# Hash attention and a PReLU feed-forward block: the weights' loads move from SyncE's queue to GpSimd's

## The chip, the cores and the metric

The kernel runs on one core of a Trainium2 chip. The metric is the device time of one execution in microseconds; less is better. Times stated without a source are positions in one profiled execution, counted from the first instruction of its span.

## The reference, cut to what matters

Two blocks follow each other: attention in which a query sees only the keys whose six hash bits equal its own, and a feed-forward block with a leaky activation (one slope per hidden unit).

```python
q_bits = (np.einsum('bhsd,dk->bhsk', q, proj) > 0)      # k_bits likewise; 6 bits each
mask = q_bucket[:, :, :, None] == k_bucket[:, :, None, :]
scores = np.where(mask, scale * (q @ k.T), -1e9)        # batch 4, heads 8, seq 768, head_dim 64
attn = softmax(scores) @ v                              # reshaped to x: 3072 x 512
h = x @ w_in                                            # 512 x 2048
out = (np.maximum(h, 0) + alpha * np.minimum(h, 0)) @ w_out   # 2048 x 512
```

The two weight matrices and alpha come as 64-bit floats; q, k, v and proj are 32-bit.

## The kernel before, in words

**Attention, up to about 326 us.** The 32 heads are handled in 16 pairs. For each pair the kernel brings q and k into a layout with head_dim on the partitions (`qT`, `kT`): the first pair by transposes on TensorE (`turn`, L695), all later ones by VectorE (`turn_blocks`, L704), from loads in four blocks for each of q and k (`load_blocks`, L512). It computes the hash bits (`hash_bits`, L730, L736), whose results GpSimd copies by DMA to their places in `qb` and `kb` (L741, L743). Then come 12 score cells (`scores`, L768): each is two small matmuls on bits and two on values, into one of three PSUM buffers of the tag "sc", followed by an exponential on ScalarE (L771) into `pt`. TensorE then multiplies with v (`attend`, L801) and sums up denominators (`totals`, L815) from `accd`. VectorE adds the exponentials up (L779 to L790) for that, and divides (`divide`: L831 reads the sums, L843 and L849 form x, which is stored to `x_s` by L850). GpSimd moves four small pieces of reciprocals in between (L840, L841).

**Weights, beside attention.** The 32 pieces of the two weight matrices, 128 x 512 elements of 64 bits (512 KB), are loaded during attention, two for each pair, and turned into 32-bit floats. `load_weight(i)` (L578 to L582) issues the load into one of three buffers (tag "raw", `bufs=3`). `weight_abs(i)` (L596 and L600 on ScalarE, or L598 on VectorE) reads it first, then `weight_clamp` and `weight_parts` (L606, L612), and `weight_sum` (L637, L640) is its last reader, so that a buffer comes free when L637 ends. `weight_group` stores finished pieces (`w_out_r`, L651) or combines four of them on GpSimd (L659, begun by a small copy to `late_sum`, L676) and stores them (`w_in_s`, L664).

**Feed-forward, from about 326 us to the end.** Matmuls of seven products per step (`Product`, L902), with weights and x read back from DRAM by SyncE (L864, L880, L979). Early in this part GpSimd loads and stores eight pieces `wo` of 512 KB (L989, L996).

**What sets the order.** Instructions wrapped in `do(...)` keep program order on their engine. DMA issues are placed by the scheduler; each engine's queue is then worked off in order, so that one whose buffer is not free holds all those behind it. The chain of calls around the change in each round `pi` (`i = 2 * pi`) is: scores, `divide` of the pair before, `weight_sum(i)`, `load_weight(i + 3)`, `weight_sum(i + 1)`, `load_weight(i + 4)`, hash bits of the next pair, `attend`, `totals`, `weight_abs(i + 2)`, loads of the pairs ahead, `weight_abs(i + 3)`. On ScalarE both `weight_abs` stand before the exponentials of the next pair. Ahead of the loop, `load` of the second pair's q and k (L1148, L1149) comes before `load_weight(0)` (L1150), and `weight_abs(0)` before the rest of the first pair's scores. In SyncE's queue before the change all q, k, v blocks but four, the weights' loads and all stores of the attention part stand in one row.

Of the kernel before, what the change touches and what calls it, by code (L numbers as in the profile page):

```python
# [349 lines left out]
def kernel(  # L350
# [48 lines left out]
    keep = ctx.enter_context(tc.tile_pool(name="keep", bufs=1))  # L399
    flag = keep.tile([1, 1], mybir.dt.int32, name="flag")  # L400
    fast_path(*args, flag)
    again = tc.nc.values_load(flag[0:1, 0:1])
    with tc.If(again > 0):
# [4 lines left out]
def fast_path(  # L408
# [12 lines left out]
    nc = tc.nc  # L421
# [61 lines left out]
    def load(pi, name):  # L483
        b, hp = pairs[pi]
        src = {"q": q, "k": k, "v": v}[name]
        if name == "v":
            t = pool.tile([P, 2, NC * D], F32, name=f"vn{pi}", tag="vn")
            nc.sync.dma_start(t, src[b, 2 * hp : 2 * hp + 2].rearrange("h (p c) d -> p h (c d)", c=NC))
            nat[name, pi] = t
        elif pi and name in BY_BLOCKS:  # L490
            load_blocks(pi, name)
        else:
            load_part(pi, name, slice(0, NC), nc.sync)

    def load_part(pi, name, cs, queue):
        b, hp = pairs[pi]
        src = {"q": q, "k": k}[name]
        if cs.start == 0:
            nat[name, pi] = pool.tile([P, NC, 2, D], F32, name=f"{name}n{pi}", tag=f"{name}n", bufs=3)
        for s in range(2):  # L500
            queue.dma_start(nat[name, pi][:, cs, s], src[b, 2 * hp + s].rearrange("(p c) d -> p c d", c=NC)[:, cs])
# [3 lines left out]
    def load_blocks(pi, name):  # L505
        b, hp = pairs[pi]
        src = {"q": q, "k": k}[name]
        nat[name, pi] = t = pool.tile([P, NC * 4, 32], F32, name=f"{name}n{pi}", tag=f"{name}n", bufs=3)
        for s in range(2):
            for h in range(2):  # L510
                a = D * s + 32 * h
                nc.sync.dma_start(  # L512
                    t[a : a + 32].rearrange("i (c u) d -> i c u d", u=4),
                    src[b, 2 * hp + s, :, 32 * h : 32 * h + 32].rearrange("(u i c) d -> i c u d", u=4, c=NC),
                )
# [39 lines left out]
    raw, wx, wr = {}, {}, {}  # L555
# [3 lines left out]
    def piece(i):  # L559


        if i < HW:
            n, m = divmod(i, 4)
            c, kk = divmod(n, 2)
            o, j = kk + 2 * (m // 2), c + 2 * (m % 2)
            return moe_w_in[o * P : (o + 1) * P, j * 512 : (j + 1) * 512]
        n, m = divmod(i - HW, 2)
        o = n + NI * m
        return moe_w_out[o * P : (o + 1) * P]
# [5 lines left out]
        ahead = (i + 1) * HW // TURNS > HW - len(left[0])  # L575
        order.append(left[0 if left[0] and ahead or not left[1] else 1].pop(0))

    def load_weight(i):  # L578
        if i < NW:
            i = order[i]  # L580
            raw[i] = pool.tile([P, 512], moe_w_in.dtype, name=f"raw{i}", tag="raw", bufs=3)
            nc.sync.dma_start(raw[i], piece(i))  # L582

    def halves(i):
        words = raw[i].bitcast(U32).rearrange("p (f t) -> p f t", t=2)
# [97 lines left out]
    def two_banks(name):  # L683
        return psum.tile([P, 2, 512], F32, name=name, tag="sc", bufs=3)
# [3 lines left out]
    def turn(pi, name, halves=BOTH, engine=None):  # L688

        src = nat[name, pi].rearrange("p c h d -> p c (h d)")  # L690
        if halves.start == 0:
            tr[name, pi] = pool.tile([P, S], F32, name=f"{name}T{pi}", tag=f"{name}T")
        ps = two_banks(f"tp_{name}{pi}")
        for c in range(CH * halves.start, CH * halves.stop):
            do(PE.transpose(ps[:, c // CH, c % CH * P :][:, :P], src[:, c], ident))  # L695
        dst = tr[name, pi].rearrange("p (h w) -> p h w", h=2)[:, halves]
        if engine is DVE:
            do(DVE.tensor_copy(dst, ps[:, halves, :CW]))
        else:
            do(ACT.activation(dst, ps[:, halves, :CW], AF.Copy, scale=DOWN if name == "q" else 1.0))  # L700
# [12 lines left out]
    def hash_bits(pi, halves=BOTH, engine=None):  # L713

        if halves.start == 0:
            bits["q", pi] = qbs[pi % 2]
            kb = pool.tile([P, 3 * CW], BF16, name=f"kb{pi}", tag="kb", bufs=1)
            bits["k", pi] = kb[:, :S]  # L720
            bits["raw", pi] = kb.rearrange("p (a w) -> p a w", w=CW)
        ps = {"k": two_banks(f"hs{pi}")}
        ps["q"] = psum_av.tile([P, 2, 512], F32, name=f"hsq{pi}", tag="av") if engine is DVE else ps["k"]
        for half in range(halves.start, halves.stop):
            for name in "qk" if engine is DVE else "kq":
                for s in range(2):
                    r, c = D * s, D * (s ^ half) + 32 * "kq".index(name)

                    for t, c in [("k", c)] + ([("q", c ^ D)] if engine is DVE and name == "q" else []):
                        do(PE.matmul(  # L730
                            ps[t][c : c + 32, half if t == "k" or engine is not DVE else 0, :CW], wh[r : r + D],
                            tr[name, pi][r : r + D, half * CW : (half + 1) * CW], start=True, stop=True,
                        ))
        if engine is None:
            raw = bits["raw", pi]
            do(ACT.activation(raw[:, 0:3:2], ps["k"][:, :, :CW], AF.Sign, bias=hb))  # L736
            for half in range(2):
                for s in range(2):
                    c = D * (s ^ half)
                    cols = slice(half * CW, (half + 1) * CW)  # L740
                    nc.gpsimd.dma_start(bits["q", pi][D * s : D * s + 32, cols], raw[c + 32 : c + 64, 2 * half])  # L741
                    if half:
                        nc.gpsimd.dma_start(bits["k", pi][D * s : D * s + D, cols], raw[c : c + D, 2])  # L743
            return
        for half in range(halves.start, halves.stop):
            cols = slice(half * CW, (half + 1) * CW)
            for s in range(2):
                c = D * (s ^ half ^ (engine is DVE)) + 32
                do(ACT.activation(
                    bits["q", pi][D * s : D * s + 32, cols], ps["q"][c : c + 32, 0 if engine is DVE else half, :CW], AF.Sign, bias=hb[c : c + 32],  # L750
                ))

            for to, c, n in [(0, 0, P)] if half == 0 else [(0, D, D), (D, 0, D)]:
                dst, src = bits["k", pi][to : to + n, cols], ps["k"][c : c + n, half, :CW]
                do(DVE.tensor_scalar(
                    dst, src, hb_k[c : c + n, 0:1], hb_k[c : c + n, 1:2], op0=ALU.is_gt, op1=ALU.subtract,
                ))
# [384 lines left out]
    for half in (first, second):  # L1142
        turn(0, "q", half)
        turn(0, "k", half, DVE)
        if half is first:
            nil[0]()
            hash_bits(0, first, DVE)
    load(1, "q")  # L1148
    load(1, "k")  # L1149
    load_weight(0)  # L1150
    load(0, "v")
    for i in range(1, 3):
        load_weight(i)
# [14 lines left out]
    for pi in range(NPAIR):  # L1168
        i = 2 * pi
# [13 lines left out]
        weight_sum(i)  # L1183
        weight_group(i)
        load_weight(i + 3)
        if pi == 0:
            weight_abs(1, DVE)
# [136 lines left out]
```

## Time and profile before

| | |
|---|---|
| median of 3 runs | 882.17 us (881.49 to 883.12) |
| the profiled execution's own time | 882.06 us |
| its span, first to last instruction | 880.2 us |
| busy TensorE matmul / weight load | 863.0 us (98%) / 576.0 us (65%) |
| busy VectorE | 749.2 us (85%) |
| busy ScalarE | 368.0 us (42%) |
| busy GpSimd | 96.8 us (11%) |
| mean granted TensorE clock | 0.993 |
| DMA moved | 137.23 MB, 156 GB/s over the span |
| share of the DMA engines' time, q1 (SyncE) / q0 (GpSimd) / q10 (ScalarE) | 49.5% / 3.9% / 0.5% |
| weights' loads | 32 from SyncE, 512 KB each, landing 3.7 to 7.1 us after issue, median 4.8 |
| hash bits' copies from GpSimd | 90, of 24 or 48 KB, landing 1.6 to 5.8 us after issue |
| an ordinary pair of the attention part | 19.15 us |

How to read it: PE is TensorE, DVE VectorE, ACT ScalarE, POOL GpSimd, SP SyncE; a "q" behind the name (SPq) is the engine's instruction queue, where DMAs are issued. A name such as L768 is a line of the kernel, and "sc<-qT,kT" is output and inputs by the program's names. The idle time before an instruction is put down to the one whose end released it. The DMA share is the mean busy share of the core's 16 DMA engines, and can exceed 1 where packets overlap.

### The profile page before, as it was taken

How to read it: one execution, taken by the hardware profiler on the slowest of the kernel's cores; microseconds unless marked ns; L12 is line 12 of the kernel's file. 1: busy time of each engine (PE TensorE's matmuls, PEld its weight loads, DVE VectorE, ACT ScalarE, POOL GpSimd, SP SyncE). 2: the span in 40 equal slices, each digit the busy share in tenths (PEclk: the TensorE clock that was granted, in tenths of full speed). 3: DMA queues.
4: the chain of work that ended last, by engine and by line, in shares of the span. 5: the costliest groups of instructions: out<-in, count | busy, mean ns of one | idle time of the engine just before them, and what ended most of it. 6: DMA issues, size and time to landing. Idle time of an engine off the chain costs nothing.

```text
span 880.2 us, 15210 instructions
## 1 busy us (share of the span) xinstructions
PE 863.0 (98%) x5706; PEld 576.0 (65%) x5706; DVE 749.2 (85%) x1215; ACT 368.0 (42%) x654; POOL 96.8 (11%) x220
## 2 busy tenths in 40 slices
PE   8999999999998999999999999999999999999996
PEld 3444444444443445559996558996557997557996
DVE  5999999999997978899888769898668988668986
ACT  6886888887766752221112222112222112222111
POOL 1221423323322311120000000000000000000000
PEclk9999999999998999999999999999999999999998
DMA  8866797797796347586433425334434333520242
GB/s 197 183 152 136 181 241 157 169 253 192 177 252 169 118 150 263 203 303 223 133 132 90 172 86 197 115 113 125 141 123 155 136 123 96 177 86 1 96 151 69
DMA packets 170819, 137.23 MB, mean 156 GB/s; under 512 B 126016, under 2 KB 154384, under 8 KB 167152
## 3 DMA queue, kind: packets, MB, share of 16 engines
q1 hardware_dynamic: 163136, 123.64, 49.5%
q0 software_dynamic: 5184, 11.34, 3.9%
q10 hardware_dynamic: 2416, 1.18, 0.5%
q8 instruction: 47, 0.77, 0.4%
q14 instruction: 36, 0.29, 0.1%
HBM read 104.87 MB, written 28.31 MB: 151 GB/s over the span
## 4 chain that ended last, share of the span: by engine, by line
PE 92%; DVE 3%; DMA 2%; issue 1%; ACT 1%; SPq 1%; ACTq 0%; DVEq 0%
PE sc L768 15%; PE av L801 13%; PE f_0a L902 2%; PE z_4a L902 2%; PE z_7a L902 2%; PE z_3a L902 2%; PE z_6a L902 2%; PE z_5a L902 2%; PE z_1a L902 2%; PE z_2a L902 2%; PE f_4a L902 2%; PE f_7a L902 2%; PE f_6a L902 2%; PE f_5a L902 2%; PE f_3a L902 2%; PE f_2a L902 2%
## 5 line engine op out<-in xcount | busy, mean ns | idle before, releaser
L771 ACT ACTIVATE pt<-sc 128x768 f32<-128x768 f32 x192 | 154.0, 812 | 8.3 <-PE sc L768 6.8
L768 PE MATMUL sc<-qT,kT 64*128 64x384 f32 x768 | 157.3, 488 | 0.0
L801 PE MATMUL av<-pt,vn 128*32 128x385 f32 (+1 forms) x1536 | 127.4, 486 | 0.0
L801 PEld LDWEIGHTS av<-pt,vn 128*32 128x32 f32 x1536 | 48.7, 109 | 77.5 <-issue 69.3
L768 PEld LDWEIGHTS sc<-qT,kT 64*128 64x128 f32 x768 | 69.3, 190 | 38.4 <-issue 38.1
L768 PE MATMUL sc<-qb,kb 64*128 64x384 bf16 x384 | 63.8, 328 | 8.0 <-ACT pt L771 7.0
L955 DVE TENSOR_TENSOR g<-g,g 128x384 f32<-128x384 f32 x128 | 68.3, 554 | 2.2
L1019 DVE TENSOR_TENSOR gs<-g,gs 128x768 f32<-128x768 f32 x56 | 53.3, 951 | 1.0
L1011 DVE TENSOR_TENSOR ws<-wl 128x512 f32<-128x512 f32 x56 | 38.4, 686 | 18.2 <-DMA wl<-w_out_s 16.3
L1019 DVE TENSOR_TENSOR gs<-g 128x768 f32<-128x768 f32 x56 | 53.2, 951 | 0.0
L596 ACT ACTIVATE wr<-raw 128x512 int32<-128x512 uint32 x32 | 22.1, 692 | 59.1 <-issue 30.2
L741 POOL DMA_DIRECT2D qb<-kb x60 | 30.1, 505 | 146.3 <-ACT kb L736 146.3
L768 PEld LDWEIGHTS <-kb 64*128 64x128 bf16 x384 | 19.6, 95 | 38.7 <-issue 14.1
L779 DVE TENSOR_TENSOR accp<-pt,pt 128x1536 f32<-128x1536 f32 x16 | 28.2, 1760 | 17.9 <-ACT pt L771 17.9
L951 DVE SCALAR_TENSOR_TENSOR g<-h,alpha 128x384 f32<-128x384 f32 x32 | 19.7, 616 | 25.2 <-ACT h L944 25.1
L784 DVE TENSOR_TENSOR accd<-accd,pt 128x1536 f32<-128x1536 f32 x16 | 28.1, 1758 | 1.7
L790 DVE TENSOR_TENSOR accd<-accd,accp 128x1536 f32<-128x1536 f32 x16 | 28.1, 1758 | 0.6
L787 DVE TENSOR_TENSOR accp<-accp,pt 128x1536 f32<-128x1536 f32 x16 | 28.0, 1753 | 0.0
L783 DVE TENSOR_TENSOR accd<-pt,pt 128x1536 f32<-128x1536 f32 x16 | 28.0, 1750 | 0.0
L902 PE MATMUL f_0a<-x,wi 128*128 128x384 f32 x64 | 23.5, 489 | 0.0
L902 PE MATMUL f_1a<-x,wi 128*128 128x384 f32 x64 | 23.3, 486 | 0.0
L902 PE MATMUL f_2a<-x,wi 128*128 128x384 f32 x64 | 23.3, 486 | 0.0
(355 smaller groups left out, 1740.2 us busy)
## 6 DMA issues: line engine op xcount, KB each, us to landing
wi<-w_in_s SPq DMA_DIRECT2D x32, 896.0 KB, 4.7
wl<-w_out_s SPq DMA_DIRECT2D x16, 1024.0 KB, 4.8
wl<-w_out_r SPq DMA_DIRECT2D x12, 1024.0 KB, 5.0
raw<-in_moe_w_out_dram SPq DMA_DIRECT2D x16, 512.0 KB, 4.9
raw<-in_moe_w_in_dram SPq DMA_DIRECT2D x16, 512.0 KB, 4.5
w_in_s<-wsi SPq DMA_DIRECT2D x16, 448.0 KB, 5.7
qn<-in_q_dram SPq DMA_DIRECT2D x64, 96.0 KB, 5.4
vn<-in_v_dram SPq DMA_DIRECT2D x16, 384.0 KB, 5.6
```

Of the source, the lines that this page charges most:

```text
L741: nc.gpsimd.dma_start(bits["q", pi][D * s : D * s + 32, cols], raw[c + 32 : c + 64, 2 * half])
L768: do(PE.matmul(sc[:, s, :CW], what["k", pi][r, ks], what["q", pi][r, qs], start=first, stop=not first,))
L771: do(ACT.activation(pts[kc][:, g, :, :CW], sc[:, :, :CW], AF.Exp, scale=SCALE / DOWN))
L779: do(DVE.tensor_tensor(accp[pi], p(0), p(1), op=ALU.add))
L783: do(DVE.tensor_tensor(accd[pi], p(3), p(4), op=ALU.add))
L784: do(DVE.tensor_tensor(accd[pi], accd[pi], p(5), op=ALU.add))
L790: do(DVE.tensor_tensor(accd[pi], accd[pi], accp[pi], op=ALU.add))
L801: do(PE.matmul(av[pi][D * s + t : D * s + t + 32, g, :w], nat["v", pi][:, s, kc * D + t : kc * D + t + 32], pts[kc][:, g, s, :w], start=(k ...
L902: do(PE.matmul(self.ps[bank], self.left(left, k), self.right(right, k), start=start and k == 0, stop=k == self.nk - 1, skip_group_check=no ...
L955: do(DVE.tensor_tensor(new_g(b, to)[:, i], g_m[b, x][:, i], g_m[b, y][:, i], op=ALU.subtract))
L1011: do(DVE.tensor_tensor(t, w2[b, n, x], w2[b, n, y], op=op))
L1019: do(DVE.tensor_tensor(t, g2[b, n, x], g2[b, n, y], op=ALU.subtract))
```

## The change

`load_weight` gets a parameter for the issuing engine, with GpSimd as its default. The first weight's load is issued by SyncE and stands before the loads of the second pair's blocks of q and k; it stood behind them. All other weights' loads keep their place in the program and go to GpSimd's queue.

```diff
-    def load_weight(i):
+    def load_weight(i, queue=nc.gpsimd):
         if i < NW:
             i = order[i]
             raw[i] = pool.tile([P, 512], moe_w_in.dtype, name=f"raw{i}", tag="raw", bufs=3)
-            nc.sync.dma_start(raw[i], piece(i))
+            queue.dma_start(raw[i], piece(i))
...
+    load_weight(0, nc.sync)
     load(1, "q")
     load(1, "k")
-    load_weight(0)
     load(0, "v")
     for i in range(1, 3):
         load_weight(i)
```

In the changed program, GpSimd's queue has 31 more DMA issues and SyncE's 31 fewer; TensorE, VectorE and ScalarE have the same instructions in the same order. In GpSimd's queue the loads 1, 2 and 3 stand after its memsets and before the first hash-bit copies; later the load `i + 3` stands before the six hash-bit copies of a round, and the load `i + 4` after them.

## The prediction

> **What bounds the kernel now.** I read five views: the busy shares, TensorE's waits, the chain of waits, the stretches pair by pair, and the timeline of each engine around what they showed. TensorE is busy 863.0 of 880.2 us, so little can be gained outside its idle time, and its waits are few (columns: who waited, for whom, total us, times, longest):
>
> ```profile
> PE sc L768 <- ACT pt L771: 7.0, 2, 4.3
> PE sc L768 <- DVE st L831: 1.0, 2, 0.8
> ACT wr L596 <- DMA raw<-in_moe_w_out_dram: 11.8, 2, 9.1
> ```
>
> ScalarE takes its work in order: the conversion of a raw weight (L596) stands before the exponentials (L771) which free TensorE's score banks. Twice the weight is late, and exponentials and scores wait behind it. The timeline shows both (start, duration, in brackets the idle time before):
>
> ```profile
> 15.23 0.67 ACT L596 ACTIVATE wr<-raw 128x512 int32<-128x512 uint32 x1 [2.68 <-DMA raw<-in_moe_w_out_dram]
> 16.65 0.34 PE L768 MATMUL sc<-qb,kb 64*128 64x384 bf16 x2 [2.68 <-ACT pt L771]
> ...
> 267.15 0.66 ACT L596 ACTIVATE wr<-raw 128x512 int32<-128x512 uint32 x1 [9.10 <-DMA raw<-in_moe_w_out_dram]
> 269.11 0.51 PE L768 MATMUL sc<-qb,kb 64*128 64x384 bf16 x2 [4.28 <-ACT pt L771]
> ```
>
> Why the second weight is late is in SyncE's queue. Its buffer was free at 251.4, when VectorE ended L637 (started 250.71), but SyncE issued the load only at 259.96, behind key blocks, stores of w_in_s and a store of x:
>
> ```profile
> 250.71 0.68 DVE L637 SCALAR_TENSOR_TENSOR wx<-raw,wx 128x512 uint32<-128x512 uint32 x1
> ...
> 247.39 6.25 SPq L512 DMA_DIRECT2D kn<-in_k_dram  x4
> 253.74 4.23 SPq L664 DMA_DIRECT2D w_in_s<-wsi  x4
> 258.07 1.80 SPq L850 DMA_DIRECT2D x_s<-x  x1
> 259.96 2.85 SPq L582 DMA_DIRECT2D raw<-in_moe_w_out_dram  x2
> ```
>
> The stretches show the price: this pair took 26.47 us, an ordinary one 19.15, and the clock was 0.87 (first number the stretch, then PE, PEld, DVE, ACT and POOL busy, last PE clock, DMA share, GB/s).
>
> ```profile
> 222.65:241.80 19.15, 19.15 (x202) 9.09 (x204) 18.20 (x26) 15.40 (x23) 7.07 (x16) 1.00 0.74 188
> 262.00:288.47 26.47, 22.02 (x202) 10.51 (x202) 20.64 (x28) 16.38 (x24) 6.86 (x14) 0.87 0.72 179
> ```
>
> **What the Trainium skill says.** "TensorE: Matmul & The Clock Gate", Part 1, says that an idle window of about 3.4 us throttles the array to half clock. The trace agrees: after 4.28 us of idleness the next four score cells took 5.80 us at a granted clock of 0.55; after 2.68 us the clock stayed at 1.00. "DMA: Bandwidth & Descriptors", SWDGE vs HWDGE vs iDMA, says that loads issued by GpSimd feed another internal queue of each DMA engine than SyncE's, and that the engine alternates between them. The page lists them as q0 and q1; how they share is not shown. "SBUF — State Buffer", SBUF: two separate sides, warns that VectorE in some modes keeps GpSimd from writing its descriptors. Here that is small: all 60 qb issues took 496 to 663 ns beside a VectorE that is busy over 90% of a pair.
>
> **The change, part by part.** The order of instructions on TensorE, VectorE and ScalarE stays as it is; 31 of 32 weight loads leave SyncE's queue for GpSimd's, and the first is put ahead of eight block loads.
>
> 1. *The late stall goes.* GpSimd is idle from 246.1 to 254.76, so it issues that load at about 251.4. A load from GpSimd of the same 512 KB (wo, w_out_s) holds it 0.76 us and lands 4.5 to 5.0 us after issue where nothing queues with it, and a median of 6.8 with wo in batches; SyncE's raw loads land in 3.7 to 7.1. With 6.8 it lands at 258.2; with the worst single value, 11.9 us (four wo loads at once), at 263.3, which would keep some 2 us of the stall but not its slow clock. ScalarE comes to it at 258.05 but also waits for VectorE's L640 (wr is double buffered) until 261.4, so the likely value is no DMA wait. What goes: the score cell due at 264.66 (pitch 0.81) began at 269.11, 4.45 us; the next four took 5.80 instead of 3.23, 2.57 us. Sum 7.0.
>
> 2. *Part of it comes back.* VectorE's sum of x (L874) stands before L831, which frees the third score bank. At 242.18 it took 1.56 us and held the third cell until 244.36 instead of 243.35: 1.0 us. In the pair after the stall the same sum (1.57 us at 287.06) was hidden, since VectorE ran ahead of a slowed TensorE. Without the stall it costs 1.0 again. Bounds 0 and 1.6. Late part: -6.0.
>
> 3. *The start.* The first weight is issued at 5.1 instead of 10.73 and two more by GpSimd at about 2.9 (end of its memsets), so the weight is there when ScalarE comes to it at 12.55, and the 2.68 us go. But the second pair's key blocks come behind 3 x 512 KB. At the 354 to 360 GB/s of the 335 to 345 us stretch that is 4.4 us of DMA time; about 1.2 us fit into the gaps at 4 to 7 us (shares 0.67, 0.49, 0.66), some 1 us more because the blocks are limited by SyncE's issue (0.70 us each at a share near 0.9). SyncE's own step adds 0.70; by the instruction order of the changed program the last key block also waits for the first weight to have landed, since its semaphore is used again. So the keys, which landed at 14.17, come 0.7 to 3.0 later; I take 1.5. VectorE transposes them (L704) before its sums of pair 0; of 1.5 it can absorb 0.49, its idle time before L779 at 17.34. Its L831 then ends at 32.8 instead of 31.79, where TensorE's third cell of the second pair began at 32.6. So the first stall turns into a wait for VectorE: cost 0.2; bounds -1.3 (keys not late at all) and +1.7. A delay of the first pair's second half of q (needed at 7.16) of up to 2.5 us hides under this.
>
> 4. *GpSimd's own queue.* Two issues of 0.5 to 0.76 us per pair. The one after L637 of the even weight (97.20 in the pair shown) ends before ScalarE releases the qb copies at 100.3. The one after the odd weight (106.6) ends at 107.35, before late_sum at 107.45; even 0.5 later it is covered, since the rr copies end at 111.97 and VectorE wants them at 113.73. What counts is the DMA queue: qb and kb copies now stand behind a raw load issued some 3 us earlier. First qb copy issued at 100.57, needed by the scores at 107.77: 7.2 us; its row said 1.6/3.6/5.8 us to landing. The raw load has 1.5 to 4 us left when qb queues, and most of that passes within the slack. I take 0; bounds 0 and 1 us per pair.
>
> 5. *SyncE's queue.* Blocks of q are no longer held by a weight's wait. No engine waited for these in mid-kernel, so nothing gained. After 326 us TensorE runs without gaps; that part only moves.
>
> Sum against the profiled execution, 882.06 us (span 880.2 and 1.9 around it; 0.1 below the median of 882.17): 882.06 - 7.0 + 1.0 + 0.2 = 876.3 us.
>
> **The rivals.**
> *Both ends gain:* keys not late and no new wait on L874: 882.06 - 7.0 - 1.3 = 873.8. For it: DMA shares of 1.18 and 1.40 at 19 to 21 us, when large and small packets were mixed. Against: a share of 0.99 over 10 to 20 us. Chance 0.15.
> *Half:* the start costs 1.7 and the late region, still at a DMA share over 0.9, gives another 1 to 1.5 us of waits: about 879.3. For it: VectorE is 97% busy (19.51 of 20.20 us) from 241.8 to 262. Chance 0.15.
> *The wait only moves:* the GpSimd load is just as late, 882. Against: 8.5 us of SyncE's queue disappear. Chance 0.05.
> *Slower, qb behind raw:* copies of bits queue behind 512 KB in the one GpSimd queue and reach the scores late. Each us beyond the slack of 7.2 us costs a us in up to 15 pairs, so from 0.4 us per pair it eats the gain; with 0.7 it is 882.06 - 6 + 10.5 = 886.6. For it: landings up to 5.8 us where the DMA engines are saturated. Against: the median of 3.6, and that a raw load is mostly through by then. Chance 0.10.
>
> **How the numbers follow.** The forecast has 0.55, the rest as given. 0.2% is 1.8 us, about what a measurement can tell here. Faster: 0.55 + 0.15 + nearly all of 0.15 = 0.84; same 0.06; slower 0.10. The range takes in the two cases beside the forecast, 873.6 to 880.4, and leaves out 0.15.
>
> **What would show it.** L596 with no DMA wait near 15 and 267; the pair at 262 back near 19.5 and its clock at 1.00; a wait for L831 near 32 and 282; kT (L704) starting at 15 to 17 instead of 14.17; qb landing below 7 us. I am wrong if scores wait for qb or kb copies, if L596 waits for a load from GpSimd, or if the granted clock drops again.

## The result, and the profile after

The changed kernel takes 879.32 us (median of 7 runs, 879.06 to 880.09) where the kernel before takes 882.17 (7 runs, 881.49 to 883.91): a ratio of 0.9966, 95% interval 0.9954 to 0.9978, 2.85 us less. Its profiled execution took 879.32 us with a span of 877.4. The forecast was 876.3.

TensorE's waits of the kernel after (columns as before: who waited, for whom, total us, times, longest):

```profile
PE tp_q L695 <- DMA qn<-in_q_dram: 4.1, 1, 4.1
PE sc L768 <- DVE st L831: 2.3, 3, 1.3
```

The line that carried the prediction, 7.0 us of L768 for L771, is gone altogether. In its place stands a wait that was 0.3 us before: the transposes of the first pair's q wait 4.1 us for their block. The third line of before, L768 for L831, has grown from 1.0 to 2.3.

The timeline of the kernel after shows the late end first: the load leaves GpSimd at 254.41 and ScalarE converts the weight at 264.04 without a wait for a DMA (267.15 before, after one of 9.10). (The releaser in the first bracket is inferred; VectorE's L637, which frees the buffer, ended at 253.84.)

```profile
254.41 0.57 POOL L582 DMA_DIRECT2D raw<-in_moe_w_out_dram  x1 [5.83 <-ACT pt L771]
...
264.04 0.68 ACT L596 ACTIVATE wr<-raw 128x512 int32<-128x512 uint32 x1 [3.56 <-issue]
...
266.30 0.34 PE L768 MATMUL sc<-qb,kb 64*128 64x384 bf16 x2 [0.18 <-DVE st L831]
...
286.91 0.34 PE L768 MATMUL sc<-qb,kb 64*128 64x384 bf16 x2 [1.29 <-DVE st L831]
```

The pair that took 26.47 us at a clock of 0.87 before now takes 19.50: the next pair's first score cell is at 283.83 instead of 288.40, 7.02 us earlier once the shift of 2.45 us between the two executions ahead of it is taken off. The last line is new: one pair later VectorE's sum of x (L874, 1.61 us from 284.68) holds the third cell for 1.29 us.

The start, in GpSimd's and TensorE's timelines of the kernel after; the last line is the same transpose in the kernel before:

```profile
2.81 0.69 POOL L582 DMA_DIRECT2D raw<-in_moe_w_in_dram  x1
3.50 0.55 POOL L582 DMA_DIRECT2D raw<-in_moe_w_out_dram  x1
...
10.72 0.67 PE L695 MATMUL tp_q<-ident,qn 128*128 128x128 f32 x3 [4.06 <-DMA qn<-in_q_dram]
```

```profile
7.19 0.52 PE L695 MATMUL tp_q<-ident,qn 128*128 128x128 f32 x3 [0.29 <-DMA qn<-in_q_dram]
```

The same start in stretches, the kernel before first (stretch, length, PE, PEld, DVE, ACT and POOL busy with counts, granted clock, DMA share, GB/s):

```profile
4.00:5.00 1.00, 0.89 (x5) 0.55 (x5) 0.00 (x0) 0.22 (x1) 0.00 (x0) 1.00 0.67 126
5.00:6.00 1.00, 0.96 (x9) 0.41 (x11) 0.55 (x1) 0.49 (x1) 0.00 (x0) 1.00 0.49 112
6.00:7.00 1.00, 0.90 (x12) 0.14 (x4) 0.06 (x2) 0.36 (x1) 0.00 (x0) 1.00 0.66 131
```

```profile
4.00:5.00 1.00, 0.98 (x7) 0.70 (x7) 0.00 (x0) 0.32 (x2) 0.06 (x1) 1.00 0.98 202
5.00:6.00 1.00, 0.96 (x13) 0.35 (x13) 0.56 (x1) 0.38 (x1) 0.00 (x0) 1.00 1.02 294
6.00:7.00 1.00, 0.66 (x10) 0.00 (x0) 0.29 (x1) 0.56 (x1) 0.00 (x0) 1.00 0.82 244
...
11.00:12.00 1.00, 1.00 (x8) 0.67 (x7) 0.00 (x0) 0.49 (x1) 0.00 (x0) 0.50 1.29 131
12.00:13.00 1.00, 1.00 (x7) 0.60 (x6) 0.56 (x1) 0.00 (x0) 0.00 (x0) 0.50 0.45 58
```

SyncE issued the second half of q at 3.96 (4.06 before), so nothing was late in its queue. The block itself, 196 KB, came 3.5 us later (10.72 against 7.19), while the DMA engines, half idle before at 5 to 6 us, were full: the 1 MB that GpSimd had asked for at 2.8 and 3.5 landed at 8.3 and 9.7. After 4.06 us without work TensorE ran at half clock for 3 us and more.

The first score cell of the second pair, in the kernel before and after:

```profile
30.96 0.34 PE L768 MATMUL sc<-qb,kb 64*128 64x384 bf16 x2
```

```profile
33.38 0.34 PE L768 MATMUL sc<-qb,kb 64*128 64x384 bf16 x2
```

It began 2.42 us later: the start costs that much where it was to be nearly free. The sum is 3.53 us for the late block and 1.57 for the half clock (the second score cell is 5.10 us later, 14.78 against 9.68), less 2.68 for the first wait of before, which fell away.

So the sum of after is +2.42 at the start, nothing in the middle (the shift stays 2.4 and an ordinary pair takes 19.15 us in both), and -5.56 at the late end (7.02 less 1.46 for L874), together -3.1 at the first matmul of the feed-forward part (322.19 against 325.30). The spans differ by 2.8: the feed-forward part took 0.3 us more.

### The profile page after: what moved, and what is told of

Same layout as the page of the kernel before. It is cut to its first block, busy times and chain, and to the rows that moved or that the text cites. A ratio compares the mean times of both kernels' runs of the same rounds, so it can differ in the third digit from the quotient of the medians.

```text
span 877.4 us, 15248 instructions
## 1 busy us (share of the span) xinstructions
PE 861.8 (98%) x5706; PEld 574.8 (66%) x5706; DVE 749.7 (85%) x1215; ACT 368.5 (42%) x654; POOL 117.6 (13%) x251
## 3 DMA queue, kind: packets, MB, share of 16 engines
q0 software_dynamic: 9648, 27.60, 10.7%
## 4 chain that ended last, share of the span: by engine, by line
PE 63%; DVE 5%; issue 1%; POOL 0%; ACT 0%; DVEq 0%; ACTq 0%
PE f_0a L902 2%; PE z_4a L902 2%; PE z_7a L902 2%; PE z_3a L902 2%; PE z_6a L902 2%; PE z_5a L902 2%; PE f_4a L902 2%; PE f_3a L902 2%; PE f_2a L902 2%; PE f_1a L902 2%; PE z_2a L902 2%; PE f_5a L902 2%; PE sc L768 2%; PE av L801 2%; PE z_1a L902 2%; PE f_7a L902 2%
## 5 line engine op out<-in xcount | busy, mean ns | idle before, releaser
L771 ACT ACTIVATE pt<-sc 128x768 f32<-128x768 f32 x192 | 154.2, 812 | 6.8 <-PE sc L768 5.3
L768 PE MATMUL sc<-qT,kT 64*128 64x384 f32 x768 | 155.8, 484 | 0.0
L768 PEld LDWEIGHTS sc<-qT,kT 64*128 64x128 f32 x768 | 68.3, 188 | 37.9 <-issue 37.7
L768 PE MATMUL sc<-qb,kb 64*128 64x384 bf16 x384 | 63.1, 324 | 2.3 <-DVE st L831 2.3
L596 ACT ACTIVATE wr<-raw 128x512 int32<-128x512 uint32 x32 | 22.2, 693 | 53.1 <-issue 36.3
L768 PEld LDWEIGHTS <-kb 64*128 64x128 bf16 x384 | 19.1, 94 | 33.2 <-issue 6.4
L779 DVE TENSOR_TENSOR accp<-pt,pt 128x1536 f32<-128x1536 f32 x16 | 28.1, 1758 | 11.2 <-ACT pt L771 11.2
```

The lines of the kernel that those rows point to most:

```text
L768: do(PE.matmul(sc[:, s, :CW], what["k", pi][r, ks], what["q", pi][r, qs], start=first, stop=not first,))
L771: do(ACT.activation(pts[kc][:, g, :, :CW], sc[:, :, :CW], AF.Exp, scale=SCALE / DOWN))
L779: do(DVE.tensor_tensor(accp[pi], p(0), p(1), op=ALU.add))
```

## The experiments

Each changes the preamble or one place of the changed kernel, or of the kernel before where that is said. Times are medians; the ratio is to the kernel before on the same chip. The theory: the late loads win some 5.6 us because they no longer stand in SyncE's queue, and the two loads that GpSimd issues at the very start lose 2.4 to 3 of them because they take the DMA engines from the first pair's q. The rivals: moving the first load is what harms; the late stall went only because everything was shifted; the order alone, not the queue, did the work.

| kernel | us (lowest to highest, runs) | ratio [95% interval] |
|---|---|---|
| after | 879.32 (879.06 to 880.09, 7) | 0.9966 [0.9954, 0.9978] |
| e1_late_only | 876.82 (876.49 to 878.96, 6) | 0.9947 [0.9932, 0.9962] |
| e2_first_early | 877.07 (876.00 to 878.08, 6) | 0.9947 [0.9932, 0.9961] |
| e3_two_early | 880.13 (879.25 to 881.89, 18) | 0.9978 [0.9970, 0.9986] |
| e4_all_sync | 881.46 (880.73 to 883.09, 14) | 0.9997 [0.9988, 1.0006] |
| e5_one_early | 877.72 (877.15 to 878.54, 6) | 0.9947 [0.9933, 0.9961] |
| e6_gated | 882.22 (880.23 to 884.63, 14) | 0.9995 [0.9985, 1.0005] |
| e7_stores_gpsimd | 881.15 (879.84 to 884.63, 22) | 0.9990 [0.9981, 0.9999] |
| e8_sums_moved | 873.89 (873.30 to 874.50, 5) | 0.9903 [0.9888, 0.9919] |
| e9_same_queue | 881.64 (879.69 to 883.01, 22) | 0.9989 [0.9982, 0.9997] |
| e10_sums_late | 875.98 (874.45 to 877.21, 6) | 0.9928 [0.9914, 0.9942] |
| e11_small_packets | 880.74 (879.95 to 883.70, 12) | 0.9988 [0.9976, 1.0000] |
| e12_sums_late_2 | 875.53 (873.87 to 876.38, 6) | 0.9923 [0.9907, 0.9938] |

### One part at a time: e1 to e4

e1: the first three loads as in the kernel before, the rest from GpSimd.

```diff
-    load_weight(0, nc.sync)
     load(1, "q")
     load(1, "k")
+    load_weight(0, nc.sync)
     load(0, "v")
     for i in range(1, 3):
-        load_weight(i)
+        load_weight(i, nc.sync)
```

> Loads 0, 1 and 2 as before (SyncE, first one behind the second pair's blocks); only the loads from 3 on are GpSimd's. Theory (the two early GpSimd loads took the DMA engines from the first pair's q and cost 2.4 us; the later ones win 5.6 by leaving SyncE's queue): TensorE meets q near 7.2 us, the first 2.7 us wait for L596 is back, the late one gone: 882.2 - 5.6 = 876.6. First rival (the first load ahead of the blocks did the harm): also 876.6, since it is undone here too. Second rival (the late stall went only because everything was shifted by the start): 881 to 882.

e2: only loads 1 and 2 go back to SyncE (the last line of that diff). e3: only the first load goes back to its old place (the first lines). e4: every load goes back to SyncE, and the first stays early (`queue=nc.sync` as the default).

> As the changed kernel, but loads 1 and 2 stay in SyncE's queue behind the first v. Theory: q near 7.2 us, no wait for L596 near 15, the second pair's keys about 1 us later than before, TensorE's third score cell of the second pair at 31.8 to 32.6: 875.8 to 876.6. First rival (the first load ahead of the blocks does the harm): 879 as in the changed kernel. Second rival: 881 to 882.

> As the changed kernel, but the first load stands behind the second pair's blocks again. Theory: q comes at 10 to 11 us as in the changed kernel and TensorE's clock drops; the first weight may land late on top of it: 879 to 880.5. First rival: the start is as before, 876.6.

> The first load is moved ahead, all 32 loads stay in SyncE's queue. Theory: the first wait goes into one for VectorE (gain 0 to 0.8), the late stall stays with its 4.3 us and its slow clock: 881.4 to 882.2. First rival: 884 to 885. If the order of the first loads alone settled the late stall: near 876.

In e1's timeline the start is that of before (its q is transposed at 7.33, L596 waits 2.31 us for the first load) and the late stall is gone all the same, so it did not go through the shift. In e4 the stall is there with all its cost, which is the order without the queue:

```profile
PE sc L768 <- ACT pt L771: 4.1, 1, 4.1
```

In e3's timeline q is late by itself, with the first load at its old place, so the first load is not what harms:

```profile
11.24 0.87 PE L695 MATMUL tp_q<-ident,qn 128*128 128x128 f32 x3 [3.82 <-DMA qn<-in_q_dram]
```

e2's timeline shows what the early first load is worth when q is left alone, VectorE's first, then TensorE's:

```profile
15.05 0.98 DVE L704 STREAM_TRANSPOSE kT<-kn 128x768 f32<-128x768 f32 x1 [1.97 <-DMA kn<-in_k_dram]
```

```profile
28.73 0.86 PE L815 MATMUL sm<-accd,ones 128*32 128x192 f32 x16 [0.53 <-DVE accd L790]
31.95 0.34 PE L768 MATMUL sc<-qb,kb 64*128 64x384 bf16 x2 [0.65 <-DVE st L831]
```

The 2.68 us wait for the weight is gone, the keys are transposed 0.9 us later than in before (14.17), and VectorE takes the wait's place: the third score cell is at 31.95 instead of 32.58, a gain of 0.6 us. That is the exchange which step 3 described. e1 and e2 have the same ratio, so this gain cannot be told in the time.

### Bytes, start or queue: e5, e6, e9, e11

e5 issues load 1 early from GpSimd and load 2 from SyncE:

```diff
-    for i in range(1, 3):
-        load_weight(i)
+    load_weight(1)
+    load_weight(2, nc.sync)
```

> As the changed kernel, but only load 1 is issued early by GpSimd; load 2 goes by SyncE after the values, and the later loads stay on GpSimd. Theory (bytes ahead): with half of the bytes beside it the first pair's second half of q comes at 8.5 to 9.3 us rather than 10.7, TensorE waits some 1.5 to 2.2 us and keeps its clock, and the time is 876.8 to 878.3 us. Rival (a fixed price for a second queue that moves large packets): q still comes after 10 us with a wait near 3.5 to 4 us, and the time is 878.8 to 880.

q comes at 8.42 after a wait of 0.95 us, and the clock stays at 1.00. Half the bytes cost 1.1 us of lateness (7.32 in e2) and all of them 3.4 to 3.9: the price is not fixed, it grows with the bytes that are beside the block, and is even smaller for the first half than I expected. This lateness of q is hidden, as step 3 said of a delay up to 2.5 us: TensorE still waits for VectorE at its third cell of the second pair (0.64 us). That cell is 1.0 us later than in e2 (32.97 against 31.95) because the second pair's keys are (transposed at 16.07 against 15.05).

e6 lets GpSimd wait for the first pair's keys before it issues loads 1 and 2, and keeps those two issues in program order behind that wait:

```diff
-            queue.dma_start(raw[i], piece(i))
+            do(queue.dma_start(raw[i], piece(i))) if 0 < first_loads[0] < 3 else queue.dma_start(raw[i], piece(i))
+            first_loads[0] += 1
...
+    do(POOL.tensor_copy(late_sum, tr["k", 0][:, S - 1 : S]))
     for i in range(1, 3):
         load_weight(i)
```

> As the changed kernel, but GpSimd copies one column of the first pair's transposed keys before it issues loads 1 and 2, so that both loads start only once those keys are in. Theory (the loads' bytes beside q cost the start): q comes within 0.3 us of the kernel before (7.2 to 7.5 us), no 4 us wait and no half clock after it; the second pair's q and k come later in exchange, so that VectorE's keys or the third score cell wait up to 1 us more; 876.3 to 877.8 us. Rival (GpSimd's queue costs the same wherever it starts, since the two loads only delay the second pair's blocks instead): the wait moves to L704 or L596 with 2 us or more, and the time is 878.5 to 880.

The loads leave at 9.10 and 9.80 and q is in time (a wait of 0.31 us), but the rival was right, and by more than it said. The timeline of VectorE, then of TensorE (lines of this kernel stand 3 further down, so L707 is L704 of before and L818 is L815):

```profile
20.16 0.98 DVE L707 STREAM_TRANSPOSE kT<-kn 128x768 f32<-128x768 f32 x1 [6.01 <-DMA kn<-in_k_dram]
```

```profile
21.28 0.51 PE L733 MATMUL hs<-kT,wh 64*32 64x384 f32 x2 [1.78 <-DVE kT L707]
33.84 1.51 PE L818 MATMUL sm<-accd,ones 128*32 128x192 f32 x16 [3.79 <-DVE accd L793]
```

Now the second pair's keys are starved, VectorE is late by 6 us, and the stall at the totals brings the half clock again (0.50 from 34 to 39 us). At 2.8 us the loads delay q, at 9.1 us they delay the second pair's keys, and here that is dearer. A place that costs nothing visible exists all the same: in e2 SyncE issues the same two loads at 12.54 and 13.05, behind the second pair's blocks and the first v.

e9 issues all three loads from SyncE ahead of the second pair's blocks:

```diff
-    load_weight(0, nc.sync)
+    for i in range(3):
+        load_weight(i, nc.sync)
     load(1, "q")
     load(1, "k")
     load(0, "v")
-    for i in range(1, 3):
-        load_weight(i)
```

> The changed kernel, but loads 1 and 2 are issued by SyncE directly behind load 0, ahead of the second pair's blocks: the same bytes move early, in the queue in which the first pair's q stands ahead of them. Theory (q was late since another queue's large packets moved beside it): q is waited for by less than 0.7 us at L695, and the second pair's k pays instead, with a wait of 4 us or more at L704 and one of 2 us or more at the totals L815; 880 to 882.5 us. Rival (the bytes alone count, whatever queue holds them): q comes after 9 us and is waited for by 2 us or more at L695.

The bytes are asked for at 5.2 to 6.6 us, behind q in the same queue: q is transposed at 7.24 without a wait, and the second pair pays, with the keys at 19.55 and 3.79 us at the totals. VectorE's wait for the keys was 3.51 us, less than the 4 expected, since another of 3.5 us for the second pair's q stands ahead of it. So q was late in the changed kernel because large transfers moved beside it, asked for from 2.8 us on in another queue. e9 also issues them 2.7 to 2.9 us later than GpSimd did, so the two reasons, the queue and the earlier moment, are not parted here.

e11 cuts each of the two GpSimd loads into two transfers of interleaved runs of 256 bytes:

```diff
-            queue.dma_start(raw[i], piece(i))
+            first_loads[0] += 1
+            if 1 < first_loads[0] <= 3:
+                cut = "p (a b c) -> p b a c"
+                for b in range(2):
+                    queue.dma_start(raw[i].rearrange(cut, b=2, c=32)[:, b], piece(i).rearrange(cut, b=2, c=32)[:, b])
+            else:
+                queue.dma_start(raw[i], piece(i))
```

> The changed kernel, but loads 1 and 2 are each cut into two transfers of interleaved runs of 256 bytes, so that the same 1 MB moves beside q in packets of q's size instead of 4 KB. Theory A (the queues take turns by packet, so large packets in the other queue are what holds q): q's second half is in by 8.0 to 9.3 us, TensorE waits under 2.5 us at L695 and keeps its clock. Theory B (the bytes or the time of the DMA engines count, whatever the packets): q comes at 10.5 us or later, with a wait of 3.8 us or more and half a clock after it. The loads themselves take longer under both, so L596 may wait for them, and the time alone does not tell the two apart: 877 to 884 us.

q is late as in the changed kernel (10.54 after 3.63 us of waiting, then half a clock), near the numbers of theory B. But the edit did not make the packets small. The DMA table of this kernel counts 9,680 packets on GpSimd's queue, that of after 9,648: 32 more, where 256-byte packets would have made some 4,000. The Trainium skill, "DMA: Bandwidth & Descriptors", Queues, rings and completion order, says that a DMA engine changes queues only after a whole packet, which holds several descriptors, the single orders to move bytes. The profile's counts by size fit such packing: all 32 extra packets are under 512 bytes, and the numbers of larger ones are those of the kernel after. So the size of what stood beside q was not changed, no run here shows how the queues take turns, and whether smaller packets would let q through stays open.

### What held the late load: e7

The kernel before, with only the stores of the rearranged weights (L664) moved to GpSimd:

```diff
-                nc.sync.dma_start(w_in_s[4 * c + ii][:, :, kk], w[:, :, ii])
+                nc.gpsimd.dma_start(w_in_s[4 * c + ii][:, :, kk], w[:, :, ii])
```

> The kernel before with one edit: the stores of the rearranged weights at L664 are issued by GpSimd instead of SyncE; all loads stay on SyncE. Theory (the late load was late since it stood in SyncE's queue behind issues that wait for the stores' data): the late load is issued near 254 to 256 us, the 4.45 us wait of L768 for L771 goes, and the time is 876 to 878.5 us. Rival (the transfers themselves fill the DMA engines there): the wait stays at 3 us or more, and the time is 881 to 882.5.

Neither was right. The timeline of SyncE's queue, the bracketed wait of TensorE below it:

```profile
244.35 10.30 SPq L512 DMA_DIRECT2D qn<-in_q_dram  x3
254.75 4.43 SPq L512 DMA_DIRECT2D kn<-in_k_dram  x4
259.28 0.60 SPq L850 DMA_DIRECT2D x_s<-x  x1
259.98 1.58 SPq L582 DMA_DIRECT2D raw<-in_moe_w_out_dram  x1
```

```profile
267.69 0.34 PE L768 MATMUL sc<-qb,kb 64*128 64x384 bf16 x2 [1.63 <-ACT pt L771]
```

The stores are gone from the queue and the load is issued at 259.98 as before (259.96): the blocks of q and k, which wait for buffers of their own, hold it just as well. It landed 1.5 us sooner (5.6 us after its issue instead of 7.1), probably since the stores were no longer beside it, which was not tested by itself. TensorE's wait fell from 4.28 to 1.63 us with no slow clock, and that of 0.18 us for L831 just ahead of it grew to 1.01. But the stores cost on their new queue. Two pairs on, in the timelines of GpSimd, VectorE and TensorE:

```profile
308.90 3.75 POOL L664 DMA_DIRECT2D w_in_s<-wsi  x4 [2.62 <-issue]
...
313.60 0.98 DVE L843 STREAM_TRANSPOSE dn<-rr 128x768 f32<-128x768 f32 x1 [2.79 <-POOL rr L841]
...
315.68 7.96 PE L801 MATMUL av<-pt,vn 128*32 128x385 f32 x96 [1.12 <-DVE x L849]
```

The four issues stand ahead of GpSimd's copies of the reciprocals (L840, L841), VectorE waits 2.79 us for those, and TensorE 1.12 us for VectorE. So a load that leaves SyncE's queue gains since *everything* in that queue stood before it, not the stores alone.

### What remains late: e8, e10, e12

e2 with the three sums of x (L874) put behind L831 to L836 on VectorE:

```diff
         weight_sums(1, vsum[pi])
+        while x_due:
+            sum_x(0, x_due.pop(0), DVE)
...
-            sum_x(0, min(pi - 11, 3), DVE)
+            if pi < 14:
+                x_due.append(pi - 11)
+            else:
+                sum_x(0, 3, DVE)
```

> The kernel of e2_first_early, but the three sums at L874 stand behind the four instructions L831 to L836 on VectorE instead of ahead of L831. Theory of step 2 (their 1.6 us hold L831 and so the third score cell): the waits of L768 for L831 in these three pairs (0.86, 0.18 and 1.29 us) go, the reader of the copy at L840 is not held, and the time is 874.3 to 875.5 us. Rival (VectorE is full in these pairs, and its work is only in another order): the wait turns up at the totals of the same pairs or one pair later, and the time is 876.5 to 877.5.

873.89 us, the fastest of all, and below the expected 874.3. TensorE's waits of this kernel have one left for L831, at the start:

```profile
PE sm L815 <- DVE accd L790: 1.4, 1, 1.4
...
PE sc L768 <- DVE st L831: 0.6, 1, 0.6
```

The totals of the late pairs begin at 241.20, 260.35, 279.49 and 298.64, 19.15 apart like an ordinary pair; in e2 they were 20.19, 19.51 and 20.59 apart. From the totals at 241.20 (240.33 in e2) to the feed-forward part it is 75.96 us instead of 78.75: the sums cost 2.8 us, not the 2.3 of the waits alone.

e10 puts the same edit on e1; e12 is e10 again.

> The kernel of e1_late_only (the first three loads where they were before the change) with the three sums moved behind L836, as in e8_sums_moved. Theory (the two edits act in different stages, and the sums' price of 2.3 to 2.8 us adds to either start): 873.6 to 874.6 us, with no wait of L768 for L831 in the late pairs. Rival (the gain of e8 needs its start): 875.5 us or more.

> The kernel of e10_sums_late once more, since its six times lay 2.8 us apart and their median above the forecast while its profiled execution met it. Theory (the edits add; the start of the kernel before, where the first load is waited for, scatters): the fastest of the runs at 873.6 to 874.6 us and a ratio of 0.991 to 0.993. Rival (the gain of e8 needs its start): a ratio of 0.993 or more, with a wait of L768 for L831 in the late pairs.

The late waits are gone in both, and both medians lie above e10's forecast of 873.6 to 874.6; by its number alone the rival was met in e10. In e12 the theory's own signs came true: the fastest run took 873.87 us, and the ratio is 0.9923. The six runs of each lie 2.8 and 2.5 us apart, the five of e8 1.2. e12's execution shows one cause. Its stretches at the wait for the first load, which e8's start doesn't have:

```profile
15.00:16.00 1.00, 0.00 (x0) 0.00 (x0) 0.62 (x2) 0.66 (x2) 0.00 (x0) 1.00 1.08 405
16.00:17.00 1.00, 0.23 (x3) 0.23 (x4) 0.93 (x3) 1.00 (x3) 0.00 (x0) 0.93 1.04 352
17.00:18.00 1.00, 1.00 (x6) 0.54 (x6) 0.55 (x1) 1.00 (x2) 0.00 (x0) 0.50 0.98 394
18.00:19.00 1.00, 1.00 (x6) 0.69 (x4) 1.00 (x1) 0.58 (x2) 0.00 (x0) 0.50 1.07 372
```

After an idle time of 2.11 us the clock halved; in e10's execution, after 1.70 us at the same place, it stayed at 1.00, and that one took 872.7 us of span against 874.6. So a wait at the start costs more in some executions than in others, and the two kernels that keep it scatter. The mean clock, which is on record for every run, fits: in both kernels the three fastest runs have 0.997 or 0.998 and the three slowest 0.996, and the 3.4 us or so that e12's stretches spend at half clock (an estimate from the means of 1 us) are 0.002 of its span. The kernel before scatters in the same way: of its 31 runs beside e1, the nine at 0.996 or 0.997 took 880.4 to 881.4 us and the four at 0.991 took 883.6 to 884.4. What a removed wait saves thus differs between executions, and the sums from the timelines hold for the profiled ones.

## Why the prediction was right, and where it wasn't

The measured 879.3 us lies within the stated 873.6 to 880.4, but close to its end: the kernel gained 2.85 us, half of the 5.8 that were forecast. That it fell inside was luck in part, since the range went that far up for the rival "half", whose reasons did not come true. The late end came out as argued; the start did not.

**Step 1, the late stall: right.** Forecast -7.0, measured -7.02. GpSimd issued the load at 254.41, which less the shift of 2.45 us is 251.96, beside the forecast 251.4, and there was no wait for it. e1 shows that the queue did this alone, and e4 that the order didn't.

**Step 2, the sum of x comes back: right, a little small.** Forecast +1.0 from the wait in an earlier pair, measured +1.46, within its bound of 1.6. The late end together was to give -6.0 and gave -5.56. e1, which changes the late loads alone, was 5.04 us faster than the kernel before on its chip (881.86), by its ratio 3.4 to 6.0 us.

**Step 3, the start: the failing step.** It had two terms. That the first wait is exchanged for one for VectorE is what e2 shows, with +0.2 forecast and -0.6 measured, in its bounds. The other was said in one sentence: a delay of the first pair's second half of q of up to 2.5 us hides. The mechanism was named and, as e5 with its 1.1 us suggests, sound; its size was neither worked out nor priced beyond the 2.5. The delay was 3.5 us, and the idle time passed into a half clock, which cost 1.6 more and had not been priced at this place. Of the 5.1 us together, 2.7 took the place of the first wait, and 2.4 remained where +0.2 was forecast. The working had counted the three loads as bytes that fill gaps and then delay the *second* pair; it had put the two from GpSimd at 2.9 us and had not set them against the block issued 1.1 us after. The gaps at shares of 0.67, 0.49 and 0.66, which it gave to these loads, were not free for them: filled to 0.98, 1.02 and 0.82, they went with 196 KB that came 3.5 us later.

**Step 4, GpSimd's own queue: right.** No score waited for qb; its copies landed in a median of 3.2 us (3.6 before), and the slower rival did not come. **Step 5, SyncE's queue: right for mid-kernel**, where every pair takes 19.15 us as before.

**The rivals.** The time, 879.3, is that of "half", but not for its reason: it had put 1.7 us on the keys of the second pair and 1 to 1.5 us on new waits at the late end. The first was 2.4 us and lay in the first pair's q, the second 0.46 beyond the forecast. The clock dropped again, which the prediction had named as a sign that it was wrong.

## What to carry to other kernels

Taking a prefetch out of an in-order issue queue is worth what stands in front of it and waits, here up to 5.6 us for one load, and moving some other entry out of the queue instead may free nothing, as the next one waits too. A prefetch that gets a queue of its own starts at once, so ask which small, urgent block is in flight at that moment: 1 MB beside 196 KB made that block 3.5 us late here. Place the first loads by what the other queues need in those microseconds, and look for what the removed stall had been hiding; here that was 2.8 us of sums ahead of the instruction that frees a bank.

## What the runs showed of the hardware that was not expected

- The half clock did not follow from the length of the idle time alone. It came with idle times of 4.06, 3.82, 3.63, 3.79 and 3.79 us (after, e3, e11, e6, e9), and not with 2.68, 2.31 or 2.70 (before, e1, e7), but it did come with 2.11 us in e12. The Trainium skill, "TensorE: Matmul & The Clock Gate", Part 1, gives an idle window of about 3.4 us; all but the last agree with it. Nor did the drop come at a fixed time: by an estimate from the mean clocks of the stretches of 1 us, it was 2.2 us after TensorE's last work in e12, 2.4 in e3 and 4.3 in the kernel after.
- On GpSimd, a copy of 32x12 values (L840, L841) took 0.18 to 0.39 us, and 1.71 and 1.80 us in two late pairs of the kernel after (at 269.15 and 289.67). Both long ones began just after VectorE's first sum of exponentials (L779, two inputs, 1.76 us from 269.04 and 289.65) and ended 0.06 us after it; e1, e2 and e3 show the same two copies beside the same sums. So the copy seems to be held until that sum ends; no run changed one of the two to show it.
